# Attention accumulators split by head and half of the queries, their copy on VectorE, another phase table and a ring of fifteen score tiles

## Chip, cores and metric

The program runs on one core of a Trainium2 chip. The metric is device time in microseconds (us), the median of several executions. One further execution was recorded by the hardware profiler; all rows below come from it.

## What is computed

Four transformer layers are applied to a sequence of 2048 tokens with 576 features, all in float32. Layers 0 and 2 are multi-head attention (32 heads of width 18), layers 1 and 3 have the same queries but one key and one value head that all 32 query heads share. The reference, cut to what matters:

```python
def _A_ref(x, wqkv, wo):              # layers 0 and 2
    qkv = (x @ wqkv).reshape(B, S, 3, H, Dh) ...
    scores = jnp.einsum("bhqd,bhkd->bhqk", q, k) * (Dh ** -0.5)
    p = softmax(scores, axis=-1)
    o = jnp.einsum("bhqk,bhkd->bhqd", p, v)
    return o.reshape(B, S, D) @ wo
def _B_ref(x, wq, wk, wv, wo):        # layers 1 and 3: k, v shared by all heads
    ...
x = x + _A_ref(_layernorm(x), A_wqkv, A_wo)
x = x + _B_ref(_layernorm(x), B_wq, B_wk, B_wv, B_wo)
x = x + _A_ref(_layernorm(x), A_wqkv, A_wo)
x = x + _B_ref(_layernorm(x), B_wq, B_wk, B_wv, B_wo)
```

## The kernel before

**Work and units.** In each layer the heads are taken in 16 pairs and the queries in four blocks of 512. A pair with a block is one *unit* here; a layer has 64 of them. Within a pair, head a=0 has its operands in partitions 0 to 63 and head a=1 in partitions 64 to 127 of `big`, so a score matmul uses only half the rows of the array, and two score matmuls of different heads can run beside each other.

A unit needs three kinds of work on TensorE (PE):
- 32 tiles of 128 queries by 512 keys for the row maximum (`psm`, `max_mm`, L653). VectorE (DVE) reduces 24 of them with L658. For four pairs of them the code forms a difference tile instead (L639), ScalarE (ACT) takes its Relu into `relu` or the free part of `xo` (L651), and DVE adds that to the partner tile and takes the maximum in one operation (L656). These maxima run 14 steps ahead of the exponentials.
- 32 tiles of 128 keys by 512 queries for the exponentials (`pse`, `exp_mm`, L879). The maxima come in as two more operand rows. ACT writes exp into an SBUF tile `pt` (L883).
- The product with the values (L921): the stationary operand is a 128 by 19 block of V with a column of ones, so 19 rows come out per head and the 19th is the softmax sum. Only 32 columns of the array are needed, so four such matmuls run side by side in four column groups. All four write one PSUM bank, `oacc`, at partitions 0, 32, 64 and 96.

**The accumulators.** Before, the four column groups are (head a, parity of the key chunk). A step of 512 columns takes four `pt` tiles (two heads, two key chunks) over all 512 queries (`pv_block`). After eight steps the unit is done: ACT copies all of `oacc` into one SBUF tile `oc` (L930). GpSimd (POOL) then adds the two parities of each head (`o_sum`, L939 and L940), the reciprocal of the sum goes through DRAM and back as rows `rb` (`l_part`, `l_inv`, `l_out`, `l_rows`), POOL multiplies (`o_mul`, L962) and the rows leave to `o_d` (`o_out`, L967).

**The order.** Nothing is scheduled by a tool here: every engine runs its instructions in the order in which the code issues them. For most of a layer that order comes from the table `UNIT`, one entry per *phase*, ten phases per unit. An entry such as `("e10 m01 e00 m12 e10 m01", 320)` means: the score matmuls named there (e for an exponential tile, m for a maximum tile, r for a difference tile; then the head; then the *rank*), and after them 320 columns of the product with V. The loop at L1043 to L1055 issues them. `PV_LAG` shifts the product against the scores, so that a unit's last columns fall at the end of the table's second entry, and its copy follows there. In the last part of each layer, when all maxima are done, another loop (L1060 to L1074) takes four exponentials and 512 columns at a time.

**Buffers.** Seven PSUM banks take the score tiles. `lru` lists them from the one handed out longest ago; the rank is the place in that list from which the next tile's bank is taken, and the matmul waits until the engine that read the bank's last tile is done. `reader` notes whether that was ACT. The `pt` tiles come from a ring of 14 buffers; `slot` chooses among those whose product with V has been issued, so that ACT need not wait for its own earlier writes. A fifteenth buffer holds `oc`.

Of the kernel before, what the change touches and what calls it, by code (L numbers as in the profile page):

```python
# [17 lines left out]
DH = D // H  # L18
# [31 lines left out]
SUM_AT = 3.75  # L50
# [5 lines left out]
O_AT = 15  # L56
SOON = (11.6, 12.6, 2.9)
# [12 lines left out]
UNIT = [("e00 m10 m02 e10 e01 e10 m00", 448),  # L70
# [9 lines left out]
UNIT = [([(o[0], int(o[1]), int(o[2])) for o in rows.split()], cols) for rows, cols in UNIT]  # L80
PV_LAG = 928
# [5 lines left out]
def tile_kernel(ctx: ExitStack, tc: tile.TileContext, A_x, A_wqkv, A_wo, B_x, B_wq, B_wk, B_wv, B_wo, out):  # L87
# [58 lines left out]
    rb = cst.tile([P, 512], F32, name="rb")  # L146
# [8 lines left out]
    reader = [False] * 7  # L155
# [302 lines left out]
    for layer in range(4):  # L458
# [125 lines left out]
        mxs, nms, pts, ocs = {}, {}, {}, {}  # L584
# [38 lines left out]
        def max_mm(bank=aged):  # L623
# [9 lines left out]
            reader[lru[-1]] = False  # L633
            b, r = 64 * a, 16 * a + 4 * qc + kb
            c0 = u * 512 + qc * P
            if (p, u) >= (0, 2) and (a, qc, kb) in m_diff:
# [9 lines left out]
                reader[lru[-1]] = True  # L646
                if not by_act:
                    seen[0] = max(seen[0], wrote.get(-1 - j, -1))
                wrote[-1 - j] = ticks[0]
# [221 lines left out]
        def exp_mm(p, u, i, rank):  # L871
# [5 lines left out]
            reader[lru[-1]] = True  # L877
            r = 64 * a
            nc.tensor.matmul(e, k[r:r + KE, kc * P:(kc + 1) * P], q[r:r + KE, u * 512:(u + 1) * 512],  # L879
                             start=True, stop=True)  # L880

            pt = pts[p, u, i] = slot(by_act)
            nc.scalar.activation(pt, e, AF.Exp, scale=SCALE)  # L883

        def slot(by_act):
            n = sum(e_next)
            if n >= 1984:
                return ptile("pt")
            if len(ring) < 14:
                ring.append(ptile("pt"))  # L890
                j = len(ring) - 1
            else:
                old = [j for j in free if wrote[j] <= seen[0]]
                j = old[0] if old and not by_act else max(free, key=lambda j: wrote[j])
                if not by_act:
                    seen[0] = max(seen[0], wrote[j])
                free.remove(j)
# [6 lines left out]
        def pv_cols(cols):  # L904

            while cols:
                n, c0 = divmod(pv_at[0], 512)
                w = min(cols, 512 - c0)
# [4 lines left out]
        def pv_block(n, c0, c1):  # L913

            p, u, i = *divmod(n // STEPS, 4), n % STEPS * 4
            cs = slice(c0, c1)
            turn[0] += 1
            for i in range(i, i + 4) if turn[0] % 2 else range(i + 3, i - 1, -1):
                a, kc = (i // 2) % 2, i // 4 * 2 + i % 2
                j = 64 * a + 32 * (kc % 2)  # L920
                nc.tensor.matmul(oacc[j:j + DH + 1, cs], v_of(kc)[:, 2 * p + a if is_a else 0, :], pts[p, u, i][:, cs],  # L921
                                 start=kc < 2 and c0 == 0, stop=kc >= 14 and c1 == 512)
                if c1 == 512:
                    pt = pts.pop((p, u, i))
                    free.extend(j for j, x in enumerate(ring) if x is pt)
            if c1 == 512 and i // 4 == STEPS - 1:
                oc = ocs[p, u] = ocs["tile"]
                ticks[0] += 1
                if m_done[0] < 4 * ns:
                    nc.scalar.activation(oc, oacc, AF.Copy)  # L930
                else:
                    copy(nc.vector, oc, oacc)


        def o_sum(p, u):
            oc = ocs.pop((p, u))
            t = sums[u % 2]
            for j in (0, 64):
                copy(nc.gpsimd, t[j:j + 32], oc[j + 32:j + 64])  # L939
            nc.gpsimd.tensor_tensor(t[:96], t[:96], oc[:96], op=OP.add)  # L940

        def l_part(p, u):
            lt = lts[p, u] = pool.tile([P, 8], F32, name="lt")
            for a in range(2):
                nc.sync.dma_start(lt[64 * a:64 * a + 64, :], sums[u % 2][64 * a + DH:64 * a + DH + 1, :])
# [9 lines left out]
        def l_rows(p, u):  # L955
            for a in range(2):
                nc.sync.dma_start(rb[64 * a:64 * a + DH, :],
                                  r_d[2 * p + a:2 * p + a + 1, u * 512:(u + 1) * 512].to_broadcast([DH, 512]))

        def o_mul(p, u):  # L960
            t = sums[u % 2]
            nc.gpsimd.tensor_tensor(t[:96], t[:96], rb[:96], op=OP.mult)  # L962

        def o_out(p, u):
            for a in range(2):
                c = (2 * p + a) * DH
                nc.sync.dma_start(o_d[c:c + DH, u * 512:(u + 1) * 512], sums[u % 2][64 * a:64 * a + DH, :])  # L967
# [20 lines left out]
        for p in range(NPAIR):  # L988
            for u in range(4):
# [5 lines left out]
                for d, f in ((SUM_AT, o_sum), (L_AT, l_part), (INV_AT, l_inv), (R_AT, l_out), (RB_AT, l_rows),  # L995
# [40 lines left out]
        ocs["tile"] = ptile("oc")  # L1036

        def exp_next(a, rank=0):
            pu, kc = divmod(e_next[a], NCH)
            exp_mm(*divmod(pu, 4), kc // 2 * 4 + 2 * a + kc % 2, rank)  # L1040
# [3 lines left out]
        while m_done[0] < 4 * ns:  # L1044
            rows, cols = UNIT[phase % len(UNIT)]
            run_todo(LEAD + sum(e_next) / 4)
            for kind, a, rank in rows:
                if kind == "e":
                    exp_next(a, rank)
# [10 lines left out]
        while sum(e_next) < 4 * ns:  # L1060
# [3 lines left out]
            left, c = 4 * ns - sum(e_next), -pv_at[0] % (512 * STEPS)  # L1064
# [11 lines left out]
        for st in range(ns, ns + L_AT + 1):  # L1076
            run_todo(LEAD + st)
            if st < ns + OUT_AHEAD:
                next(outs)
                pv_cols(512 * ns - pv_at[0] - (0 if st > ns else 512))  # L1080
# [33 lines left out]
```

## Time and profile before

| | |
|---|---|
| Time, median of 3 runs (lowest to highest) | 5524.15 us (5523.9 to 5525.74) |
| Span of the profiled execution, first to last instruction | 5520.9 us |
| Granted TensorE clock | 1.000 |
| POOL busy | 1839.9 us (33%) |
| DMA, share of 16 engines, main queue | 18.7% |

The three runs carry some 3 to 5 us around the span. In the profile's rows, PE is a matmul and PEld the load of its stationary operand; a row of a timeline has the start, the time from the first start to the last end, the engine, line, operation, tiles, shapes and count. The profile counts each matmul of the product with V as two instructions, one behind the other: four matmuls of 320 columns, one for each column group, are a row with x8.

### The profile page before, as it was taken

To read this page: it belongs to the slowest core of one execution; us is meant where nothing else is said; L and a number is where in the kernel's file an instruction comes from. 1 tells how busy PE (TensorE), PEld (TensorE's weight loads), DVE (VectorE), ACT (ScalarE), POOL (GpSimd) and SP (SyncE) were. 2 spreads that over 40 slices of the span, in tenths; PEclk is the share of its full clock that TensorE was granted. 3 is DMA by queue.
4 is the path that set the end of the run, shared out by engine and by line. 5 is a ranking of instruction groups with operands and counts; after the bars stand their busy time and mean duration, and the time that the engine had idled before them with its cause. 6 is when DMAs were issued, how large, how long until landed. Compare 5 with 4: busy or idle time off the path is not lost.

```text
span 5520.9 us, 143086 instructions
## 1 busy us (share of the span) xinstructions
PE 5509.2 (100%) x55774; PEld 3050.7 (55%) x55774; DVE 4920.3 (89%) x9493; ACT 4889.3 (89%) x9882; POOL 1839.9 (33%) x2382
## 2 busy tenths in 40 slices
PE   9999999999999999999999999999999999999999
PEld 8655555454855555555686555545458545454546
DVE  4799999998799999999637999999977999999995
ACT  3599999999299999999626999999992999999996
POOL 3243333334233323233412433333342333333332
PEclk9999999999999999999999999999999999999999
DMA  6321111111411000001243211111114111010002
GB/s 219 119 60 45 45 45 48 43 45 34 136 57 31 24 24 21 24 21 25 64 176 109 58 49 43 45 46 48 40 43 133 54 28 25 24 25 21 24 15 84
DMA packets 277610, 306.04 MB, mean 55 GB/s; under 512 B 136434, under 2 KB 194378, under 8 KB 267642
## 3 DMA queue, kind: packets, MB, share of 16 engines
q1 hardware_dynamic: 276930, 296.89, 18.7%
q8 instruction: 437, 7.16, 0.5%
q14 instruction: 243, 1.99, 0.1%
HBM read 169.68 MB, written 123.13 MB: 53 GB/s over the span
## 4 chain that ended last, share of the span: by engine, by line
PE 97%; issue 1%; DVE 1%; ACT 1%; DMA 0%; POOL 0%; SPq 0%; POOLq 0%; ACTq 0%
PE oacc L921 38%; PE pse L879 27%; PE psm L653 17%; PE psn L275 7%; PE psq L481 5%; PE psm L639 3%; DVE mx L658 1%; ACT pt L883 1%; PE ps L261 0%; POOL ev L494 0%; DMA m_d<-tr 0%; DMA qk_d<-ev 0%; PE oacc L262 0%; DMA big<-m_d 0%; DMA big<-qk_d 0%
## 5 line engine op out<-in xcount | busy, mean ns | idle before, releaser
L883 ACT ACTIVATE pt<-pse 128x512 f32<-128x512 f32 x8192 | 4185.0, 612 | 10.1 <-PE pse L879 1.9
L658 DVE TENSOR_REDUCE mx<-psm 128x1 f32<-128x512 f32 x6208 | 3942.4, 684 | 88.6 <-PE psm L653 66.3
L879 PE MATMUL pse<-big 64*128 64x512 f32 x8192 | 2280.5, 432 | 0.5 <-DMA big<-m_d 0.5
L653 PE MATMUL psm<-big 62*128 62x512 f32 x7200 | 2158.9, 443 | 2.2 <-ACT evr L493 0.8
L879 PEld LDWEIGHTS pse<-big 64*128 64x128 f32 x8192 | 1174.4, 184 | 1064.2 <-ACT pt L883 758.2
L921 PE MATMUL oacc<-pt,vbuf 128*19 128x32 f32 (+11 forms) x26544 | 1728.2, 368 | 0.3 <-ACT oc L930 0.2
L653 PEld LDWEIGHTS psm<-big 62*128 62x128 f32 x7200 | 878.2, 184 | 204.3 <-DVE mx L658 75.9
L921 PEld LDWEIGHTS oacc<-pt,vbuf 128*19 128x19 f32 x26544 | 533.9, 98 | 819.9 <-issue 661.4
L186 POOL TENSOR_SCALAR hl<-neg 128x8 fp32r<-128x8 f32 x256 | 50.6, 198 | 2462.2 <-DVE neg L854 2462.2
L921 PE MATMUL oacc<-pt,vy 128*19 128x288 f32 (+3 forms) x8176 | 566.3, 383 | 0.0
L949 POOL TENSOR_TENSOR rl<-lt,mone 128x8 f32<-128x8 f32 x256 | 422.0, 1648 | 320.0 <-DMA lt<-os 318.1
L656 DVE CUSTOM_DVE_ANT_0 relu<-psm,relu 128x512 f32<-128x512 f32 x496 | 342.9, 691 | 76.3 <-ACT pt L883 50.9
L186 POOL TENSOR_SCALAR os<-oc 32x512 f32<-32x512 f32 x512 | 315.3, 616 | 102.4 <-DVE oc L186 50.6
L656 DVE CUSTOM_DVE_ANT_0 xo<-psm,xo 128x512 f32<-128x512 f32 x496 | 332.1, 670 | 15.5 <-ACT pt L883 1.6
L490 ACT ACTIVATE ev<-psq 128x512 fp32r<-128x512 f32 (+1 forms) x112 | 66.9, 597 | 311.5 <-PE psq L481 222.4
L940 POOL TENSOR_TENSOR os<-os,oc 96x512 f32<-96x512 f32 x256 | 330.6, 1291 | 21.4
L962 POOL TENSOR_TENSOR os<-os,rb 96x512 f32<-96x512 f32 x256 | 327.9, 1281 | 23.1 <-DMA rb<-r_d 23.1
L921 PEld LDWEIGHTS oacc<-pt,vy 128*19 128x19 f32 x8176 | 189.8, 98 | 242.0 <-issue 197.7
L651 ACT ACTIVATE xo<-psm 128x512 f32<-128x512 f32 x496 | 317.1, 639 | 0.0
L275 PE MATMUL psn<-wsm,xx 128*128 128x288 f32 x2240 | 310.4, 297 | 0.1
L275 PEld LDWEIGHTS psn<-wsm,xx 128*128 128x128 f32 x2240 | 299.0, 188 | 15.4 <-issue 13.1
L651 ACT ACTIVATE relu<-psm 128x512 f32<-128x512 f32 x496 | 303.6, 612 | 0.0
(102 smaller groups left out, 2781.3 us busy)
## 6 DMA issues: line engine op xcount, KB each, us to landing
big<-qk_d SPq DMA_DIRECT2D x172, 432.0 KB
qk_d<-ev SPq DMA_DIRECT2D x96, 512.0 KB
qk_d<-ev SPq DMA_DIRECT2D x120, 256.0 KB
rb<-r_d SPq DMA_DIRECT2D x512, 36.0 KB
o_d<-os SPq DMA_DIRECT2D x512, 36.0 KB
o<-o_d SPq DMA_DIRECT2D x56, 256.0 KB
xx<-qk_d SPq DMA_DIRECT2D x120, 72.0 KB
big<-m_d SPq DMA_DIRECT2D x512, 4.0 KB
```

The costliest lines, as they stand in the source:

```text
L186: eng.tensor_scalar(dst, src, 1.0, 0.0, op0=OP.mult, op1=OP.add)
L275: nc.tensor.matmul(ps, lhs[:, xc, :], wsm[:, wc, h * 288:(h + 1) * 288], start=i == 0, stop=i == len(TERMS) - 1)
L651: nc.scalar.activation(t, ps, AF.Relu)
L653: nc.tensor.matmul(ps, q[b:b + KM, c0:c0 + P], k[b:b + KM, kb * 512:(kb + 1) * 512], start=True, stop=True)
L656: nc.vector.tensor_tensor_reduce(t, ps, t, 1.0, LOWEST, OP.add, OP.max, mx[:, r:r + 1])
L658: nc.vector.reduce_max(mx[:, r:r + 1], ps, axis=AX.X)
L879: nc.tensor.matmul(e, k[r:r + KE, kc * P:(kc + 1) * P], q[r:r + KE, u * 512:(u + 1) * 512], start=True, stop=True)
L883: nc.scalar.activation(pt, e, AF.Exp, scale=SCALE)
L921: nc.tensor.matmul(oacc[j:j + DH + 1, cs], v_of(kc)[:, 2 * p + a if is_a else 0, :], pts[p, u, i][:, cs], start=kc < 2 and c0 == 0, stop=k ...
L940: nc.gpsimd.tensor_tensor(t[:96], t[:96], oc[:96], op=OP.add)
L949: nc.gpsimd.tensor_tensor(rl, lts.pop((p, u)), mone, op=OP.pow)
L962: nc.gpsimd.tensor_tensor(t[:96], t[:96], rb[:96], op=OP.mult)
```

## The change

The four column groups become (head a, half of the unit's 512 queries). A step takes two `pt` tiles (two heads, one key chunk) over 256 columns, each tile's two halves going to two groups, and a unit now has 16 such steps. Each group's accumulator is then complete over all keys, with 256 columns, so `o_sum` and the tile `oc` fall away. DVE copies `oacc[:, :256]` straight into `sums`. The sums' load becomes one DMA, the rows' store four of half the length, and `rb`, `o_mul` work on 128 partitions by 256. The table `UNIT` has other entries; the ring has 15 tiles; `reader` holds the number of ACT's last read instead of yes or no, and `slot` uses it.

The core of the diff:

```diff
+RING = 15
 UNIT = ...
-        ("m10 e00 m11 m00 e10 e01", 480),
-        ("e10 m01 e00 m12 e10 m01", 320),
-        ("e10 e01 r10 m00", 256),
+        ("e01 m11 e00 m12 e00 e10", 384),
+        ("m00 e10 m01 e10 r00 m10", 448),
+        ("e10 m01 r02 m11 e00 e11 m00", 416),
...
-PV_LAG = 928
+PV_LAG = 832
...
-            if len(ring) < 14:
+            if len(ring) < RING:
...
                 old = [j for j in free if wrote[j] <= seen[0]]
-                j = old[0] if old and not by_act else max(free, key=lambda j: wrote[j])
-                if not by_act:
+                new = [j for j in free if seen[0] < wrote[j] <= by_act]
+                if new:
+                    j = max(new, key=at_)
+                elif old and (by_act >= 0 or first or len(old) > 1):
+                    j = max(old, key=at_)
+                else:
+                    j = max(free, key=at_)
                     seen[0] = max(seen[0], wrote[j])
...
-            for i in range(i, i + 4) if turn[0] % 2 else range(i + 3, i - 1, -1):
-                a, kc = (i // 2) % 2, i // 4 * 2 + i % 2
-                j = 64 * a + 32 * (kc % 2)
-                nc.tensor.matmul(oacc[j:j + DH + 1, cs], v_of(kc)[:, 2 * p + a if is_a else 0, :], pts[p, u, i][:, cs],
-                                 start=kc < 2 and c0 == 0, stop=kc >= 14 and c1 == 512)
+            groups = [(a, h) for a in range(2) for h in range(2)]
+            for a, h in groups if turn[0] % 2 else groups[::-1]:
+                j = 64 * a + 32 * h
+                nc.tensor.matmul(oacc[j:j + DH + 1, c0:c1], v_of(kc)[:, 2 * p + a if is_a else 0, :],
+                                 pts[tiles[a]][:, 256 * h + c0:256 * h + c1],
+                                 start=kc == 0 and c0 == 0, stop=kc == NCH - 1 and c1 == 256)
...
-                if m_done[0] < 4 * ns:
-                    nc.scalar.activation(oc, oacc, AF.Copy)
-                else:
-                    copy(nc.vector, oc, oacc)
+                copy(nc.vector, sums[u % 2][:, :256], oacc[:, :256])
-        def o_sum(p, u):
-            for j in (0, 64):
-                copy(nc.gpsimd, t[j:j + 32], oc[j + 32:j + 64])
-            nc.gpsimd.tensor_tensor(t[:96], t[:96], oc[:96], op=OP.add)
```

How the order of instructions changes, at the places of which the prediction speaks. First PE, before: from the third entry of the table (its 320 columns begin a new unit in `oacc`) through the fourth and fifth.

```order
L879 MATMUL pse<-big 128x512
L653 MATMUL psm<-big 128x512
L879 MATMUL pse<-big 128x512
L653 MATMUL psm<-big 128x512
L879 MATMUL pse<-big 128x512
L653 MATMUL psm<-big 128x512
L921 MATMUL oacc<-pt,vbuf 19x320 x4
L879 MATMUL pse<-big 128x512 x2
L639 MATMUL psm<-xx,big 128x512
L653 MATMUL psm<-big 128x512
L921 MATMUL oacc<-pt,vbuf 19x192 x4
L921 MATMUL oacc<-pt,vbuf 19x64 x4
```

PE with the change, from the last score matmul of the third entry through the fourth: the first 256 columns begin a new unit.

```order
L652 MATMUL psm<-big 128x512
L927 MATMUL oacc<-pt,vbuf 19x256 x4
L927 MATMUL oacc<-pt,vbuf 19x192 x4
L877 MATMUL pse<-big 128x512
L652 MATMUL psm<-big 128x512
L639 MATMUL psm<-big 128x512
L652 MATMUL psm<-big 128x512
L877 MATMUL pse<-big 128x512 x2
L652 MATMUL psm<-big 128x512
L927 MATMUL oacc<-pt,vbuf 19x64 x4
L927 MATMUL oacc<-pt,vbuf 19x256 x4
L927 MATMUL oacc<-pt,vbuf 19x96 x4
```

The entry with four score matmuls is gone; the entries now have six or seven. A run of columns is cut wherever it crosses a multiple of 256 instead of 512, so a unit's 4096 columns come in 23 pieces instead of 17.

ACT before, around a unit's end (`oc<-oacc` is the copy, the rows of `relu` and `xo` are difference tiles):

```order
L651 ACTIVATE relu<-psm 128x512
L883 ACTIVATE pt<-pse 128x512 x8
L930 ACTIVATE oc<-oacc 128x512
L883 ACTIVATE pt<-pse 128x512 x5
L651 ACTIVATE xo<-psm 128x512
L883 ACTIVATE pt<-pse 128x512 x2
L651 ACTIVATE relu<-psm 128x512
```

ACT with the change, around a unit's end; it lies within the first row of `pt`:

```order
L650 ACTIVATE relu<-psm 128x512
L882 ACTIVATE pt<-pse 128x512 x15
L650 ACTIVATE xo<-psm 128x512
L882 ACTIVATE pt<-pse 128x512 x8
L650 ACTIVATE relu<-psm 128x512
L882 ACTIVATE pt<-pse 128x512 x8
L650 ACTIVATE xo<-psm 128x512
```

The copy has left ACT; the difference tiles stand elsewhere among the exponentials.

DVE with the change, around the copy, which is the row with `os<-oacc` (`mx` are the maxima of this unit and the next, the rows ISA the joint operations with a Relu tile):

```order
L657 TENSOR_REDUCE mx_89<-psm 128x1 x10
L655 ISA xo,mx_89<-psm,xo 128x512
L655 ISA mx_89 128x1
L657 TENSOR_REDUCE mx_89<-psm 128x1 x7
L655 ISA relu,mx_89<-psm,relu 128x512
L655 ISA mx_89 128x1
L186 TENSOR_SCALAR os_113<-oacc 128x256
L657 TENSOR_REDUCE mx_89<-psm 128x1 x2
L657 TENSOR_REDUCE mx_90<-psm 128x1
L853 TENSOR_REDUCE neg<-mx_89 128x8
L657 TENSOR_REDUCE mx_90<-psm 128x1 x2
L655 ISA xo,mx_90<-psm,xo 128x512
```

DVE before, around the end of a set of maxima (the change of `mx` and the row `neg`), had only reduces there:

```order
L658 TENSOR_REDUCE mx_89<-psm 128x1 x4
L658 TENSOR_REDUCE mx_90<-psm 128x1
L854 TENSOR_REDUCE neg<-mx_89 128x8
L658 TENSOR_REDUCE mx_90<-psm 128x1 x4
L863 STREAM_TRANSPOSE tr<-hl_115 128x32
L656 ISA xo,mx_90<-psm,xo 128x512
L656 ISA mx_90 128x1
L658 TENSOR_REDUCE mx_90<-psm 128x1 x2
```

The copy now stands behind the reduces of the second entry and ahead of those of the third.

More of the change, by code (lines that the diff above doesn't have):

```diff
@@ L144, in tile_kernel @@
     x_d = dram.tile([len(AWAY), P, D], F32, name="x_d")
-    rb = cst.tile([P, 512], F32, name="rb")
+    rb = cst.tile([P, 256], F32, name="rb")
     sums = [cst.tile([P, 512], F32, name=f"os{i}") for i in range(2)]
@@ L152, in tile_kernel @@
         nc.gpsimd.memset(t, 0.0)
-    reader = [False] * 7
+    reader = [-1] * 7
     lru, held = list(range(7)), set()
@@ L926, in pv_block @@
-            if c1 == 512 and i // 4 == STEPS - 1:
-                oc = ocs[p, u] = ocs["tile"]
-                ticks[0] += 1
-                if m_done[0] < 4 * ns:
-                    nc.scalar.activation(oc, oacc, AF.Copy)
-                else:
-                    copy(nc.vector, oc, oacc)
-        def o_sum(p, u):
-            oc = ocs.pop((p, u))
-            t = sums[u % 2]
-            for j in (0, 64):
-                copy(nc.gpsimd, t[j:j + 32], oc[j + 32:j + 64])
-            nc.gpsimd.tensor_tensor(t[:96], t[:96], oc[:96], op=OP.add)
+            tiles = [(p, u, kc // 2 * 4 + 2 * a + kc % 2) for a in range(2)]
@@ new lines, in pv_block @@
+            groups = [(a, h) for a in range(2) for h in range(2)]
[4 more added lines that the diff above has]
+                                 start=kc == 0 and c0 == 0, stop=kc == NCH - 1 and c1 == 256)
+            if c1 == 256:
+                for t in tiles:
+                    pt = pts.pop(t)
+                    free.extend(j for j, x in enumerate(ring) if x is pt)
@@ L942, in l_part @@
+            if c1 == 256 and kc == NCH - 1:
+                copy(nc.vector, sums[u % 2][:, :256], oacc[:, :256])
         def l_part(p, u):
             lt = lts[p, u] = pool.tile([P, 8], F32, name="lt")
-            for a in range(2):
-                nc.sync.dma_start(lt[64 * a:64 * a + 64, :], sums[u % 2][64 * a + DH:64 * a + DH + 1, :])
+            nc.sync.dma_start(lt, sums[u % 2][DH::32, :256])
         def l_inv(p, u):
@@ L966, in o_out @@
                 c = (2 * p + a) * DH
-                nc.sync.dma_start(o_d[c:c + DH, u * 512:(u + 1) * 512], sums[u % 2][64 * a:64 * a + DH, :])
+                for h in range(2):
+                    j, t0 = 64 * a + 32 * h, u * 512 + 256 * h
+                    nc.sync.dma_start(o_d[c:c + DH, t0:t0 + 256], sums[u % 2][j:j + DH, :256])
         relu, raw = (pool.tile([P, 640], F32, tag="xh", bufs=2, name=n) for n in ("relu", "raw"))
@@ L1046, in tile_kernel @@
             run_todo(LEAD + sum(e_next) / 4)
-            for kind, a, rank in rows:
+            for i, (kind, a, rank) in enumerate(rows):
                 if kind == "e":
-                    exp_next(a, rank)
+                    exp_next(a, rank, i < 3)
                 elif m_done[0] < 4 * ns:
```

58 lines of the change are left out of this document (30 added, 28 removed), and 6 rows, old and new, of the table UNIT.

## The prediction

> **What bounds the kernel now.** I read the page's busy times and the chain first, then busy time by stretch, then one unit on PE instruction by instruction.
>
> ```profile
> PE 5509.2 (100%) x55774; PEld 3050.7 (55%) x55774; DVE 4920.3 (89%) x9493; ACT 4889.3 (89%) x9882; POOL 1839.9 (33%) x2382
> ...
> PE oacc L921 38%; PE pse L879 27%; PE psm L653 17%; PE psn L275 7%; PE psq L481 5%; PE psm L639 3%; DVE mx L658 1%; ACT pt L883 1%; PE ps L261 0%; POOL ev L494 0%; DMA m_d<-tr 0%; DMA qk_d<-ev 0%; PE oacc L262 0%; DMA big<-m_d 0%; DMA big<-qk_d 0%
> ```
> ```profile
> core 0: us, PE busy (x) PEld busy (x) DVE busy (x) ACT busy (x) POOL busy (x), PEclk, DMA share, GB/s
> 1000.00:1036.77 36.77, 36.77 (x404) 18.47 (x400) 35.47 (x69) 36.72 (x75) 11.58 (x14) 1.00 0.14 33
> ```
>
> The chain lies on PE by 97 parts in 100, on L921, L879 and L653. But matmuls overlap in the records, so a PE that is busy all the time proves nothing, and in a stretch of two units (36.77 us) ACT is busy for 36.72 us and DVE for 35.47 us. Three engines look full. Which of them sets the pace is seen only in the starts on PE through one unit:
>
> ```profile
> 1022.44 0.50 PE L879 MATMUL pse<-big 64*128 64x512 f32 x2
> ...
> 1023.11 0.63 PE L921 MATMUL oacc<-pt,vbuf 128*19 128x192 f32 x16
> 1023.67 0.73 PE L653 MATMUL psm<-big 62*128 62x512 f32 x3
> ...
> 1024.59 1.01 PE L921 MATMUL oacc<-pt,vbuf 128*19 128x448 f32 x16
> 1025.53 0.50 PE L653 MATMUL psm<-big 62*128 62x512 f32 x1
> ...
> 1026.66 0.95 PE L921 MATMUL oacc<-pt,vbuf 128*19 128x448 f32 x8
> 1027.54 0.50 PE L879 MATMUL pse<-big 64*128 64x512 f32 x1
> ...
> 1028.67 0.90 PE L921 MATMUL oacc<-pt,vbuf 128*19 128x32 f32 x16
> 1029.50 0.50 PE L879 MATMUL pse<-big 64*128 64x512 f32 x1
> ...
> 1030.62 0.41 PE L921 MATMUL oacc<-pt,vbuf 128*19 128x128 f32 x8
> ...
> 1031.45 0.50 PE L879 MATMUL pse<-big 64*128 64x512 f32 x1
> ...
> 1032.60 0.90 PE L921 MATMUL oacc<-pt,vy 128*19 128x224 f32 x16
> 1033.43 0.50 PE L879 MATMUL pse<-big 64*128 64x512 f32 x1
> ...
> 1034.57 0.90 PE L921 MATMUL oacc<-pt,vy 128*19 128x320 f32 x16
> 1035.40 0.49 PE L879 MATMUL pse<-big 64*128 64x512 f32 x1
> ...
> 1036.53 0.95 PE L921 MATMUL oacc<-pt,vy 128*19 128x416 f32 x16
> 1037.42 0.49 PE L653 MATMUL psm<-big 62*128 62x512 f32 x1
> ...
> 1037.75 0.40 PE L653 MATMUL psm<-big 62*128 62x512 f32 x2
> ...
> 1038.33 1.00 PE L921 MATMUL oacc<-pt,vy 128*19 128x480 f32 x8
> 1039.26 0.50 PE L879 MATMUL pse<-big 64*128 64x512 f32 x1
> ...
> 1040.16 0.73 PE L921 MATMUL oacc<-pt,vbuf 128*19 128x320 f32 x8
> 1040.83 0.50 PE L879 MATMUL pse<-big 64*128 64x512 f32 x2
> ```
>
> The unit lasts 1040.83 − 1022.44 = 18.39 us. It starts at the table's fourth entry; a row of L921 with x8 is one piece of columns, x16 is two, and the shape is the first one's. From a phase's first score matmul to its first L921: with four scores 0.67 us; with six 0.92, 0.91 and 0.90 (entries 5, 2, 3); with seven 1.13, 1.13, 1.12, 1.15, 1.14 and 1.13. Two scores of different heads run together, so these are two, three and four steps, and a seventh matmul costs as much as an eighth would. The time depends on the number of steps alone, about 0.22 us each, within 0.03 us, whatever the tiles are and whoever reads them. From L921 to the next phase: 320 columns 0.67, 448 columns 0.88, 480 columns 0.93, so 0.145 us and 0.00164 us a column. In none of the ten phases is there a wait worth more than 0.02 or 0.03 us. **PE sets the pace**; ACT and DVE are full beside it because the table feeds them just enough.
>
> **The change part by part.** *Steps.* Before: one phase with two steps, three with three, six with four: 35. The new table has six phases of six scores and four of seven, heads alternating so that each still fills its pairs: 6·3 + 4·4 = 34. Taking the means of the unit above, scores cost 0.67 + 3·0.91 + 6·1.133 = 10.20 us before and 6·0.91 + 4·1.133 = 9.99 us after: **−0.21 us a unit**.
>
> *Pieces.* Columns stay 4096 a unit, and ten changes from scores to columns and back. The cuts rise from 17 pieces to 23. What a cut costs stands in pairs of rows: 448 columns in one piece take 0.88 us (from 1026.66), 416 + 32 take 0.89 (from 1036.53); 480 in one piece 0.93, 448 + 32 take 0.94 (from 1024.59). So between 0 and 0.01 us each; I take 0.005, so **+0.03 us a unit**. That covers a piece as narrow as 32, while the new ones have 64 and more. That two groups now read one `pt` tile at two places, with the same V block, appears in no row. I cost it at nothing: the columns a group streams and their number stay the same. The Trainium skill, TensorEngine Tiling (Array Packing), section Instruction Overhead, speaks against more pieces: a matmul has about 60 cycles of overhead, and one of few columns takes as long as one of 60. If 24 more matmuls, each in two passes, paid that one after the other at 2.4 GHz (the Trainium skill, TensorE: Matmul & The Clock Gate, the table at its head), it would be an estimated 1.2 us a unit, and the time an estimated 5771 us. The trace disagrees: the cut of 0.01 us above holds eight such instructions.
>
> *The copy.* From ACT goes one row a unit; DVE gets one of half the columns.
>
> ```profile
> L930 ACT ACTIVATE oc<-oacc 128x512 f32<-128x512 f32 x248 | 148.9, 600 | 0.4 <-issue 0.4
> ...
> L369 DVE TENSOR_TENSOR xo<-psn,xo 128x288 f32<-128x288 f32 x118 | 52.2, 453 | 71.8 <-PE psn L275 70.8
> ...
> L863 DVE STREAM_TRANSPOSE tr<-hl 128x32 f32<-128x32 f32 x256 | 51.4, 201 | 3.7 <-POOL hl L858 3.7
> ...
> L186 DVE TENSOR_SCALAR oc<-oacc 128x512 f32<-128x512 f32 x8 | 5.5, 691 | 6.9 <-PE oacc L921 6.3 <-POOL rl L949 0.6
> ```
>
> DVE's price for 256 columns is not there: 0.453 us for 288 and 0.691 us for 512 bound it from above, the 0.201 us of its 128x32 transpose from below. On the line through the first two it is 0.42 us, the value I take. ACT's relief is worth nothing while PE paces. DVE's load rises from 35.47/2 = 17.74 to 18.16 us a unit. That is under the new unit of 18.21 us, but barely; the busy time overstates it, since reduces that queue overlap:
>
> ```profile
> 1022.04 1.28 DVE L658 TENSOR_REDUCE mx<-psm 128x1 f32<-128x512 f32 x2
> ...
> 1031.43 6.42 DVE L658 TENSOR_REDUCE mx<-psm 128x1 f32<-128x512 f32 x10
> ```
>
> Two in 1.28 us where one alone lasts 0.68 is 0.60 us each at full pace, and ten in 6.42 is 0.64, with small waits among them. At 0.60 for the 24 reduces and four joint operations, and 0.4 for the two small ones, DVE needs 17.2 us before and 17.6 with the copy, 0.6 us less than the unit.
>
> *The added wait.* The copy waits for the unit's last product columns and stands in DVE's line ahead of the third entry's three reduces; behind these wait the PSUM banks, and PE for them. PE itself waits for the copy before it may write `oacc` again, after the third entry's six scores: a cover of 0.91 us. Copying takes 0.42, so the copy may start 0.49 us after the columns end at no cost. Two reduces stand ahead of it from the second entry. That phase lasts 0.91 + 0.145 + 384·0.00164 = 1.69 us; its two maxima start on PE at 0 and 0.33 us (1037.42 and 1037.75 in the old second entry) and take 0.5, so a DVE without arrears reduces from 0.5 to 1.7 us. It arrives at the copy about when PE does, with 0.49 us to spare, and the wait is hidden. Before, ACT's copy of 0.60 us stood at the same place, in the same cover, and the third entry still took 0.90. The copy also waits for the stores of `sums` two units before. Here are a copy and the stores issued next:
>
> ```profile
> 1002.66 0.60 ACT L930 ACTIVATE oc<-oacc 128x512 f32<-128x512 f32 x1
> ...
> 1009.81 0.81 SPq L967 DMA_DIRECT2D o_d<-os  x2
> ```
>
> These stores free the tile which the copy one unit after 1002.66 would write, at about 1021. They have 10 us to land, so that is free.
>
> *The rest.* POOL loses three operations a unit at 33% busy. SP issues one DMA more a unit, and its queue mostly waits:
>
> ```profile
> SPq L864 <- DVE mx L656: 2309.8, 242, 11.5
> ```
>
> That is 9.5 us of waiting a time. The ring of 15 and the exact readers change which buffer ACT writes and with which waits; in the unit ACT is never what PE stands for, so nothing there. At the layers' ends the eight DVE copies shrink from 0.69 to 0.42, at most 2 us in all.
>
> *Sum.* −0.21 + 0.03 = −0.18 us a unit, 18.39 to 18.21. L930 ran 248 times, 62 times a layer; the table's loop lasts until 2048 − 56 maxima are issued, 62.25 units, so 249 units in all. 249·0.18 = 45 us. The profiled span goes from 5520.9 to 5476 us. The median of the runs, 5524.15, lies 3.25 us above the span, so **5479 us**.
>
> **Bounds of that.** If cuts cost nothing and the 1.15 and 1.14 fall to 1.12 as well, it is 0.24 a unit and 60 us, with 2 us from the ends 5462. If cuts cost 0.01 each (0.15 left) and each of three more three-step phases, which lack the spare half step, waits 0.02, it is 0.09 a unit, 22 us: 5502.
>
> **The rivals.** *Partly given back:* a seven-score phase has an empty half step that takes up a late bank, a six-score phase has none, and six phases are of that kind now. For: 1.15 and 1.14 show small waits. Against: 0.92, 0.91, 0.90 show hardly any. At 0.11 to 0.14 us a unit the gain is 11 to 17 us, 5507 to 5513.
> *Nothing:* DVE's true need is nearer its busy 18.16, plus 0.1 to 0.3 us lost around the copy. The unit stays at 18.3 to 18.45: 5513 to 5535.
> *Slower, by a late copy:* if DVE comes to the copy more than 0.49 us after the columns' end, PE stands at the third entry's columns for the excess. With one reduce still ahead that is 0.11 us, with two 0.71 and (0.71 − 0.18)·249 = +132 us, 5656. For: DVE is 96% busy. Against: the count above.
> *Slower, by the pieces:* each new one pays its load of V, unhidden:
>
> ```profile
> L921 PEld LDWEIGHTS oacc<-pt,vbuf 128*19 128x19 f32 x26544 | 533.9, 98 | 819.9 <-issue 661.4 <-ACT oc L930 91.2
> ```
>
> 6·0.098 = 0.59 us, less the 0.21: +95 us, 5619. Against: the 0.01 us of a cut, which holds such loads already.
> *ACT paces:* its 36.72 of 36.77 us taken at face value. Its copy, 0.49 us from start to start (1039.46 to 1039.95, below), goes: 248·0.49 = 122 us, 5402. Against:
>
> ```profile
> 1030.04 5.02 ACT L883 ACTIVATE pt<-pse 128x512 f32<-128x512 f32 x10
> ...
> 1039.46 0.60 ACT L930 ACTIVATE oc<-oacc 128x512 f32<-128x512 f32 x1
> 1039.95 1.57 ACT L883 ACTIVATE pt<-pse 128x512 f32<-128x512 f32 x3
> ```
>
> Ten exponentials of 0.61 in 5.02 us start 0.49 apart, so 36 rows and a copy need 18.1 of 18.39 us, and PE's phases keep their lengths. The Trainium skill, Perfetto Trace Analysis, section Identifying the Most-Contended Engine, would judge PE by its weight loads, here 55%, and name ACT; the starts on PE say otherwise.
>
> **How the numbers follow.** Forecast 0.70; partly given back 0.12; nothing 0.07; late copy 0.05; pieces 0.03; ACT paces 0.03. The first two make 0.82, and their ends are the range, 5462 to 5513. A change of 0.2% (11 us) is about what can be told from none. Faster by more: 0.70 + 0.12 + 0.03 = 0.85; within: 0.07; slower: 0.08.
>
> **What would show it.** Right: units of 18.2 us; six-score phases at 0.91 and seven-score phases at 1.13; phases of three pieces within 0.02 us of the line; the copy at about 0.42 us, with the third entry's scores still 0.90 to 0.92 ahead of L921. ACT's busy share would fall by some 2%, with no further gain. Wrong: L921 waiting for the copy; six-score phases of 1.0 us; score phases unchanged but columns slower per column, which would be the two groups on one `pt` tile.

## The result, and the profile after

| | before | after |
|---|---|---|
| Time, median (lowest to highest), four executions each | 5524.02 us (5523.12 to 5525.74) | 5493.55 us (5493.19 to 5495.69) |
| Ratio, 95% interval | | 0.9945 (0.9931 to 0.996) |
| Span of the profiled execution | 5520.9 us | 5493.8 us |
| A unit: median / mean of 244, from the starts on PE | 18.382 / 18.396 us | 18.259 / 18.281 us |
| of the mean: score matmuls / product with V | 10.218 / 8.178 us | 10.072 / 8.209 us |

The changed kernel is 30.5 us faster. The forecast was 45 us faster (5479 us), its range 5462 to 5513 us. The mean unit is 0.115 us shorter, times 249 units 28.7 us; the profiled span lost 27.1 us (the profiled execution after is the longest of its four).

The page's busy times and its chain, after:

```profile
PE 5479.3 (100%) x68190; PEld 3441.6 (63%) x68190; DVE 4944.7 (90%) x9741; ACT 4810.0 (88%) x9634; POOL 1052.3 (19%) x1614
...
PE oacc L927 38%; PE pse L877 23%; PE psm L652 21%; PE psn L275 7%; PE psq L481 6%; PE psm L639 2%; DVE mx L657 1%; PE ps L261 0%; POOL ev L494 0%; DMA m_d<-tr 0%; DMA big<-m_d 0%; DMA xx<-qk_d 0%; DMA rb<-r_d 0%; PE oacc L262 0%; SPq L553 0%
```

PE still carries the chain by 97 parts in 100, POOL went from 33% to 19%, ACT from 89% to 88%, and DVE with the copy from 89% to 90%. Busy time by stretch, for one unit:

```profile
993.69:1011.94 18.25, 18.25 (x252) 10.79 (x249) 17.85 (x36) 18.03 (x37) 2.73 (x4) 1.00 0.07 18
```

The columns are PE, PEld, DVE, ACT and POOL busy. DVE works 17.85 of 18.25 us with the copy in it, where the prediction's plain sum gave 18.16; ACT 18.03. The same unit on PE, its first score matmul and first product of entries 1, 2, 3, 6, 7 and 10, with the scores between them that matter below:

```profile
993.69 0.50 PE L652 MATMUL psm<-big 62*128 62x512 f32 x1
...
994.86 0.96 PE L927 MATMUL oacc<-pt,vy 128*19 128x64 f32 x24
995.74 0.49 PE L877 MATMUL pse<-big 64*128 64x512 f32 x1
...
996.64 0.85 PE L927 MATMUL oacc<-pt,vy 128*19 128x128 f32 x16
997.42 0.50 PE L652 MATMUL psm<-big 62*128 62x512 f32 x1
...
998.33 0.95 PE L927 MATMUL oacc<-pt,vbuf 128*19 128x256 f32 x16
...
1003.14 0.49 PE L652 MATMUL psm<-big 62*128 62x512 f32 x1
1003.15 0.73 PE L877 MATMUL pse<-big 64*128 64x512 f32 x3
1003.72 0.45 PE L652 MATMUL psm<-big 62*128 62x512 f32 x2
1004.10 0.85 PE L927 MATMUL oacc<-pt,vbuf 128*19 128x256 f32 x16
1004.88 0.49 PE L877 MATMUL pse<-big 64*128 64x512 f32 x1
...
1005.78 0.85 PE L927 MATMUL oacc<-pt,vbuf 128*19 128x128 f32 x16
...
1010.03 0.50 PE L877 MATMUL pse<-big 64*128 64x512 f32 x1
...
1010.61 0.56 PE L652 MATMUL psm<-big 62*128 62x512 f32 x2
...
1011.16 0.85 PE L927 MATMUL oacc<-pt,vy 128*19 128x192 f32 x16
```

Entry 1 (seven scores) takes 1.17 us to its first product, entries 2, 3 and 7 (six) 0.90, 0.91 and 0.90, entry 6 (six) 0.96. Over the 244 units, without the three that are about 1 us or more longer (all near a layer's start), the means are 1.176, 0.898, 0.914, 1.135, 1.128, **0.953**, 0.903, 0.909, 0.908 and 1.135 us for entries 1 to 10. The forecast had 0.91 and 1.133: **two entries are 0.043 us too long each, the rest is right.** What happens in entry 6 is seen on PEld and DVE:

```profile
1002.93 0.68 DVE L655 CUSTOM_DVE_ANT_0 relu<-psm,relu 128x512 f32<-128x512 f32 x1
...
1003.49 0.36 PEld L652 LDWEIGHTS psm<-big 62*128 62x128 f32 x2
```

The last score of entry 6 takes the bank that DVE's joint operation reads, 1002.93 to 1003.61. The second of the two loads in the last row ends at 1003.85 and lasts 0.18, so it starts at 1003.67: 0.06 us after the bank is free, and only 0.05 before its matmul at 1003.72. That matmul then lasts 0.45 and the product starts 0.38 after it. In entry 7, undisturbed, the last pair starts at 1005.45, lasts 0.39, and the product follows 0.33 behind. So the *load* carries the wait for the bank; in the trace this load waits for DVE's semaphore as its matmul does. Over all 7200 matmuls of L652, a load that starts 0.2 to 0.3 us ahead (2096 of them) goes with a duration of 393 ns, one 0.10 to 0.12 ahead (319) with 393, one 0.03 to 0.06 ahead (206) with 437, one that starts at the same time (2875, mostly an entry's first pair) with 497. So for a matmul to run at full pace its bank must be free some 0.06 + 0.105 = 0.16 us before it starts. In entry 6 it is free 0.118 us before (median), in entry 1 twice 0.14 (third and seventh score, banks that ACT reads).

Not every late bank costs time. The sixth of seven scores takes a bank that is free only 0.053 to 0.063 us before in entries 1, 4, 5 and 10, and entries 4, 5 and 10 still take 1.13 us; in the kernel before it was 0.053 to 0.056 in five entries (6 to 10), which took 1.126 to 1.154. In entry 10 above, the sixth is the second matmul of 1010.61; it starts 0.49 us ahead of the product, and with faster readers (the run that shortens both, below) 0.57 ahead, while the entry takes 1.141 in place of 1.135. An entry of seven has half a step empty, and there such a wait fits in. The prediction had looked for waits of PE and saw hardly any; such a loss stands in no list of PE's waits, only in a longer matmul and a later product.

### The profile page after: what moved, and what is told of

It reads as the page before. It is cut to its first block, busy times and chain, and to the rows that moved or that the text cites. A ratio compares the mean times of both kernels' runs of the same rounds, so it can differ in the third digit from the quotient of the medians.

```text
span 5493.8 us, 166922 instructions
## 1 busy us (share of the span) xinstructions
PE 5479.3 (100%) x68190; PEld 3441.6 (63%) x68190; DVE 4944.7 (90%) x9741; ACT 4810.0 (88%) x9634; POOL 1052.3 (19%) x1614
## 4 chain that ended last, share of the span: by engine, by line
PE 97%; DMA 1%; DVE 1%; SPq 1%; POOL 0%; issue 0%; ACT 0%; POOLq 0%; ACTq 0%; DVEq 0%
PE oacc L927 38%; PE pse L877 23%; PE psm L652 21%; PE psn L275 7%; PE psq L481 6%; PE psm L639 2%; DVE mx L657 1%; PE ps L261 0%; POOL ev L494 0%; DMA m_d<-tr 0%; DMA big<-m_d 0%; DMA xx<-qk_d 0%; DMA rb<-r_d 0%; PE oacc L262 0%; SPq L553 0%
## 5 line engine op out<-in xcount | busy, mean ns | idle before, releaser
L652 PE MATMUL psm<-big 62*128 62x512 f32 x7200 | 2361.3, 438 | 1.9 <-ACT xo L650 1.1
L877 PE MATMUL pse<-big 64*128 64x512 f32 x8192 | 2358.5, 437 | 4.0 <-DMA big<-m_d 2.9
L927 PE MATMUL oacc<-pt,vbuf 128*19 128x256 f32 (+5 forms) x34864 | 1710.2, 319 | 0.1
L652 PEld LDWEIGHTS psm<-big 62*128 62x128 f32 x7200 | 1165.9, 184 | 445.9 <-ACT pt L882 342.1
L927 PEld LDWEIGHTS oacc<-pt,vbuf 128*19 128x19 f32 x34864 | 779.6, 98 | 733.2 <-issue 429.4
L927 PE MATMUL oacc<-pt,vy 128*19 128x256 f32 (+2 forms) x12272 | 570.5, 311 | 0.0
L927 PEld LDWEIGHTS oacc<-pt,vy 128*19 128x19 f32 x12272 | 277.7, 98 | 250.7 <-issue 165.1
L496 DVE TENSOR_TENSOR ev<-psq,ev 128x512 fp32r<-128x512 f32 (+1 forms) x84 | 57.9, 691 | 205.7 <-ACT ev L490 189.8
L956 POOL TENSOR_TENSOR os<-os,rb 128x256 f32<-128x256 f32 x256 | 188.1, 735 | 151.1 <-DMA rb<-r_d 96.6
L639 PE MATMUL psm<-big 54*128 54x512 f32 x512 | 204.9, 400 | 0.1
```

What stands on the lines that cost most here:

```text
L639: nc.tensor.matmul(ps.rearrange("p (h t) -> p h t", h=2) if p == 0 or not is_a else ps, q[b:b + 3 * DH, c0:c0 + P], k, start=True, stop=True)
L652: nc.tensor.matmul(ps, q[b:b + KM, c0:c0 + P], k[b:b + KM, kb * 512:(kb + 1) * 512], start=True, stop=True)
L927: nc.tensor.matmul(oacc[j:j + DH + 1, c0:c1], v_of(kc)[:, 2 * p + a if is_a else 0, :], pts[tiles[a]][:, 256 * h + c0:256 * h + c1], start ...
L956: nc.gpsimd.tensor_tensor(t, t, rb, op=OP.mult)
```

## The experiments

Times are medians; the kernel before, run on the same chips, lay between 5524.3 and 5525.8.

### Which part of the change brings the gain

T1 was: the table alone, by its one step less. Five kernels recombine the three parts: table, accumulators, engine of the copy.

**The old table in the changed kernel.**

```diff
 UNIT = ...
-        ("e01 m11 e00 m12 e00 e10", 384),
+        ("m10 e00 m11 m00 e10 e01", 480),
...
-PV_LAG = 832
+PV_LAG = 928
```

> The change without its table: accumulators by head and half of the queries, copy on VectorE, ring of 15, but the ten phases and the lag of 928 of before. Theory T1 (the table alone brings the gain; the accumulators cost 0.03 us a unit through their six more cuts, the copy nothing): a unit of 18.38 to 18.42 us against 18.38 before, so the time stays at 5524 to 5533 us. Rival T2 (taking the copy from ScalarE or the new accumulators bring part of the gain themselves): the unit falls below 18.34 and the time below 5514. Rival T3 (the new accumulators or the copy on VectorE are what took a third of the forecast gain): the unit rises to 18.43 or more, 5536 us or more.

Measured: 5565.97 us, ratio 1.0073 (1.0061 to 1.0086), unit 18.557: T3 holds, T1 missed. The product cost 0.041 us more than before, near the 0.03 of T1, but entry 3 went from 0.906 to 0.967 and entry 5 from 0.908 to 1.013. DVE around the copy in this kernel, then the same place in the changed one:

```profile
989.85 0.69 DVE L655 CUSTOM_DVE_ANT_0 relu<-psm,relu 128x512 f32<-128x512 f32 x1
990.47 0.08 DVE L655 DVE_READ_ACCUMULATOR2_ANT mx<- 128x1 f32 x1
990.47 1.28 DVE L657 TENSOR_REDUCE mx<-psm 128x1 f32<-128x512 f32 x2
991.67 0.42 DVE L186 TENSOR_SCALAR os<-oacc 128x256 f32<-128x256 f32 x1
```
```profile
996.92 0.68 DVE L655 CUSTOM_DVE_ANT_0 relu<-psm,relu 128x512 f32<-128x512 f32 x1
997.52 0.08 DVE L655 DVE_READ_ACCUMULATOR2_ANT mx<- 128x1 f32 x1
997.64 0.42 DVE L186 TENSOR_SCALAR os<-oacc 128x256 f32<-128x256 f32 x1
```

The old second entry has three maxima, the new one two, so one reduce more stands ahead of the copy. Under the old table the copy starts 0.50 us after the third entry's first score (991.17) and ends at 992.09, 0.05 ahead of the product at 992.14; in the changed kernel it starts 0.22 after (997.42) and ends 0.27 ahead of 998.33. In entry 5 the second exponential takes a bank of DVE that is free only 0.055 us before. The prediction's rival of a late copy is real; the new table is what keeps it away.

**The accumulators alone** (old table, copy of 256 columns on ACT):

```diff
-                copy(nc.vector, sums[u % 2][:, :256], oacc[:, :256])
+                copy(nc.scalar if m_done[0] < 4 * ns else nc.vector, sums[u % 2][:, :256], oacc[:, :256])
```

> The old table and lag with accumulators by head and half of the queries and a ring of 15, the copy of 256 columns on ScalarE inside the loop. T1/T5 (accumulators cost only their six more cuts, 0.03 us a unit; a shorter copy on ScalarE, 0.2 us, is worth nothing while TensorE paces): unit 18.38 to 18.43 us, time 5524 to 5536; and the 40 us lost with the copy on VectorE under the old table are the copy's alone. Rival T3 (two groups reading one score tile, or the accumulators' layout, cost more): 5540 us or more.

Measured: 5524.72 us, 0.9998 (0.9989 to 1.0007), unit 18.390. The total is as T1/T5 had it, but it is the sum of two terms that cancel: the product took 0.044 us more a unit (T1 had 0.03), and the scores 0.042 less (T1/T5 had nothing), 0.018 of it in entry 4, whose last bank, which ACT reads, was free only 0.137 us ahead before and is 0.297 ahead here. Against the kernel before, the copy on ACT is shorter here, and the ring and the choice of buffer differ too; which of these relieved the scores was not separated. The 41 us of the kernel above are the copy on DVE under a table that was not made for it.

**The new table alone**, in the kernel before:

> The kernel before with only the new table and its lag of 832: old accumulators, copy of 512 columns on ScalarE, ring of 14. T1 (34 steps in place of 35 are the gain, the copy on VectorE and the cuts are side effects): six-score phases mostly 0.91 us, unit 18.20 to 18.28 us, time 5490 to 5505. T2 (the table only works once the copy has left ScalarE, which has 36.72 us of work in two units of 36.77 and cannot follow a shorter unit): ScalarE needs 36 rows at 0.49 us and a copy of 0.49, 18.13 us a unit, but it must do so without one idle moment, so late banks take back more than half of the 0.21 us: unit 18.30 or more, 5510 us or more.

Measured: 5711.05 us, 1.0337 (1.0322 to 1.0351), unit 19.148. T1 is refuted; T2 holds, but 187 us were not foreseen by it. Waits of PE and of PEld there:

```profile
PE oacc L921 <- ACT oc L930: 121.0, 248, 0.7
```
```profile
PEld oacc L921 <- ACT oc L930: 199.0, 248, 1.2
PEld oacc L921 <- ACT pt L883: 43.9, 258, 0.2
```

Entry 3 lasts 1.471 us, 0.56 more: the new table ends a unit with four exponentials in the second entry, the copy stands behind them on ACT, and the product behind the copy. The columns of entry 5 take 1.130 in place of 0.829: they wait for score tiles that ACT has not written, 258 times. A likely reason, not tested by itself: the old accumulators open a step with four tiles at once, the new ones with two.

**The changed kernel with its copy on ACT** (same edit as for the accumulators alone), **and the new table alone with its copy of 512 columns on DVE:**

```diff
-                if m_done[0] < 4 * ns:
-                    nc.scalar.activation(oc, oacc, AF.Copy)
-                else:
-                    copy(nc.vector, oc, oacc)
+                copy(nc.vector, oc, oacc)
```

> The changed kernel with the copy of 256 columns on ScalarE again inside the ten-phase loop. Theory T5 (the new table puts ScalarE's arrears at the unit's end: the last exponential of the second entry is read 1.40 us after its score starts; a copy there stands behind it, and TensorE at the third entry's columns behind the copy): the copy ends some 4.9 us after the unit's first score, where the columns want to begin at 4.65, so the third entry lasts 1.15 to 1.30 us in place of 0.914, with more lost after it because ScalarE is late; unit 18.5 to 18.9 us, time 5560 to 5650. Rival T6 (what costs the new table 0.9 us a unit with the old accumulators is the old accumulators, not the engine of the copy): within 10 us of the changed kernel.

> The kernel before with the new table and its lag, and the copy of the whole 512 columns on VectorE (0.69 us in place of 0.42); old accumulators, ring of 14. T5 (the copy's engine decides): the copy ends some 4.52 us after the unit's first score, still before the third entry's columns at 4.65, so the third entry stays at 0.92 to 0.95; 0.27 us more work for VectorE shows as late banks in entries 4 to 7; unit 18.26 to 18.45 us, time 5490 to 5535, so 180 to 220 us under the same table with the copy on ScalarE. T6 (the accumulators decide): 5600 us or more.

Measured: copy on ACT 5586.65 us (1.0110, 1.0094 to 1.0126), entry 3 at 1.253, unit 18.630, all inside T5's ranges. The row of PE at entry 3's product names the wait:

```profile
995.58 0.41 PE L927 MATMUL oacc<-pt,vbuf 128*19 128x256 f32 x4 [0.27 <-ACT os L184]
```

New table with old accumulators and DVE's copy: 5633.82 us (1.0195, 1.018 to 1.0209), 77 us under the same table with ACT's copy where T5 had 180 to 220, and above its range. T5 was nearly right on entry 3 (0.955, against 0.92 to 0.95), but entry 4 went to 1.345, where it had foreseen small losses. DVE there:

```profile
984.26 0.69 DVE L186 TENSOR_SCALAR oc<-oacc 128x512 f32<-128x512 f32 x1
984.87 1.88 DVE L658 TENSOR_REDUCE mx<-psm 128x1 f32<-128x512 f32 x3
```

The reduces behind the copy start 0.61 us after its start, against 0.34 in the changed kernel (997.64 to 997.98), and entry 4 stands for their banks by 0.21 us. Entry 5's columns again take 1.13, and entry 7 1.00, as in the other kernel with the old accumulators: that is T6's part. Neither theory holds alone. The whole picture ("new" accumulators include the ring of 15 and the new choice of buffer):

| table | accumulators | copy | us |
|---|---|---|---|
| old | old | ACT, 512 columns | 5524.0 |
| old | new | ACT, 256 | 5524.7 |
| old | new | DVE, 256 | 5566.0 |
| new | old | ACT, 512 | 5711.1 |
| new | old | DVE, 512 | 5633.8 |
| new | new | ACT, 256 | 5586.7 |
| new | new | DVE, 256 | 5493.6 |

**Of the seven combinations run, only the one with all three parts new gains.** The old table and accumulators with the copy on DVE, that part by itself, were not run. The steps saved are the table's, but the gain comes only with the short copy on DVE and the new accumulators beside it.

### Where the missing third went

**Maxima over 448 keys** (the kernel leaves the last 64 keys of these tiles out of the maximum).

```diff
-                    nc.vector.reduce_max(mx[:, r:r + 1], ps, axis=AX.X)
+                    nc.vector.reduce_max(mx[:, r:r + 1], ps[:, :448], axis=AX.X)
```

> The changed kernel with VectorE's plain maxima taken over 448 of the 512 keys of each tile; the last 64 keys of these tiles are left out of the row maximum. Each reduce is 64 columns shorter, about 0.07 us. T1 (in the sixth entry the last score's weight load waits for a bank that VectorE frees late; in the first entry it waits for banks that ScalarE frees): entry 6 falls from 0.953 to about 0.91 us, entry 1 stays at 1.16 to 1.18, unit 18.21 to 18.23, time about 10 us less than the changed kernel's. Rival T3 (the orders of heads in these two entries cost the time by themselves, whoever reads the banks): both stay, time within 3 us of the changed kernel's. Rival T4 (ScalarE is late everywhere because VectorE's arrears delay it): both fall.

Measured: 5491.03 us, 0.9939 (0.9926 to 0.9951), unit 18.256. Entry 6 fell to 0.907, entry 1 stayed at 1.173, as T1 said; but entry 7 rose from 0.903 to 0.944, and the 10 us did not come. (The sixth score of entry 1 had its bank 0.249 us ahead here in place of 0.055, and the entry did not change: that late bank costs nothing.) PEld's waits, in this kernel and, below, in the changed one:

```profile
PEld pse L877 <- ACT pt L882: 191.5, 910, 1.1
PEld pse L877 <- DVE mx L657: 77.8, 184, 1.0
```
```profile
PEld pse L877 <- ACT pt L882: 167.0, 714, 1.4
PEld pse L877 <- DVE mx L657: 139.7, 460, 0.4
```

Waits on DVE went down by 276 times, those on ACT up by 196. In entry 7 the last exponential takes the bank of the fourth score of entry 6, which ACT reads third in line there. In the changed kernel that bank is free 0.162 us before, just enough; with entry 6 shorter, 0.111. Two banks stood at nearly the same limit.

**32 columns moved from entry 6 to entry 5:**

```diff
-        ("m02 e11 e02 m11 e00 e11 m00", 416),
-        ("m11 e00 e12 e00 m10 m01", 384),
+        ("m02 e11 e02 m11 e00 e11 m00", 448),
+        ("m11 e00 e12 e00 m10 m01", 352),
```

> The changed kernel with 32 columns moved from the sixth entry to the fifth (448 and 352), so that the sixth entry's scores start 0.053 us later after the same banks were handed to their readers. T1 (a bank must be free some 0.16 us before the matmul that overwrites it; in entry 6 it is free 0.11 us before): entry 6 falls from 0.953 to about 0.91; entries 7 to 9 start 0.05 us earlier against the engines and may give it back, so the time is between 5483 and 5495 us. Rival T3 (entry 6 costs 0.953 by its order of heads): entry 6 stays at 0.95, the time within 2 us of the changed kernel's.

Measured: 5505.61 us, 0.9964 (0.9951 to 0.9976): outside both ranges. Entry 6 fell to 0.901, so T3 is out; entry 7 rose to 1.000. The same bank explains the size. ACT begins to read entry 6's first exponential 0.57 us after the entry's start in both kernels, so the later start gives it no lead. From the entry's start to the last exponential of entry 7 it needs, by its lags in the changed kernel, 0.338 + 1.197 to the third reading, 0.61 for it and 0.16 to the matmul: 2.30 us. PE without a wait is there after 0.901 + 0.724 + 0.578 = 2.20; 0.10 us is missing, and 0.097 was lost. So entry 7 lost nearly all that entry 6 had saved (0.052 us of scores, 0.053 of columns), and the 32 columns more in entry 5 (0.058 us) were paid besides: the unit went from 18.259 to 18.311.

**Both readers shortened:** the maxima as above, and the exponentials over 448 queries (of each tile the last 64 are left out, and old values enter the product).

```diff
-            nc.scalar.activation(pt, e, AF.Exp, scale=SCALE)
+            w = 448 if any(x is pt for x in full) else 512
+            full.append(pt)
+            nc.scalar.activation(pt[:, :w], e[:, :w], AF.Exp, scale=SCALE)
```

> The changed kernel with both readers shortened: VectorE's plain maxima over 448 of 512 keys, and ScalarE's exponentials over 448 of the 512 queries of a tile once its buffer has been filled (the last 64 keys are left out of the maximum, and for the last 64 queries of each block stale exponentials enter the product). TensorE's own instructions, their order and ranks are those of the changed kernel. T1'' (entries 1, 6 and 7 wait for banks that the two readers free late, and for nothing else; shortening VectorE alone moved the wait to a bank of ScalarE): entry 1 falls from 1.176 to 1.12-1.14 us, entry 6 from 0.953 and entry 7 stay at 0.89-0.91, unit 18.13 to 18.19 us, time 5463 to 5476: the size of the step that the forecast assumed. Rival T3' (the orders of heads or TensorE's own loads cost 0.04 us in these entries): entry 1 stays at 1.16 or more and the unit above 18.22, time above 5483.

Measured: 5465.49 us, 0.9890 (0.9874 to 0.9907), unit 18.166. Entries 1, 6 and 7 are 1.142, 0.902 and 0.900 (entry 1 has a median of 1.129; a few long ones at layers' starts lift the mean); T1'' had 1.12 to 1.14 and twice 0.89 to 0.91. T3' is out. PE at entries 6 and 7:

```profile
998.40 0.50 PE L652 MATMUL psm<-big 62*128 62x512 f32 x1
998.40 0.73 PE L878 MATMUL pse<-big 64*128 64x512 f32 x3
998.97 0.40 PE L652 MATMUL psm<-big 62*128 62x512 f32 x2
999.30 0.85 PE L930 MATMUL oacc<-pt,vbuf 128*19 128x256 f32 x16
1000.08 0.49 PE L878 MATMUL pse<-big 64*128 64x512 f32 x1
...
1000.98 0.85 PE L930 MATMUL oacc<-pt,vbuf 128*19 128x128 f32 x16
```

The last pair of entry 6 lasts 0.40 in place of 0.45 and the product follows 0.33 behind. With PE's own program unchanged, the readers were worth 0.093 us a unit, 23 of the 28 us.

### A better order, the ring, the layers' starts

**Two more tables** were laid out by a count of the readers' paces. The third one's first, fifth and sixth entries:

```diff
-UNIT = [("m00 e11 r12 m00 m10 e00 e10", 448),
+UNIT = [("m10 r00 m11 e10 m01 e11 e00", 448),
...
-        ("m02 e11 e02 m11 e00 e11 m00", 416),
-        ("m11 e00 e12 e00 m10 m01", 384),
+        ("e10 m00 e00 e11 m00 m10 r00", 448),
+        ("e00 m10 m11 e01 m00 e10", 384),
```

> The changed kernel with a third table: again six entries of six scores and four of seven, and 4096 columns at the same lag, but orders and ranks laid out so that, by a count of the readers' own paces (one exponential in 0.48 us, one maximum in 0.60) and of 0.16 us from a bank's release to the matmul that overwrites it, no entry waits more than 0.02 us, save the first with 0.04. Theory T1' (what the changed kernel lacks of the forecast 0.21 us is the late banks of entries 1 and 6, and with them entry 7, nothing else): entry 6 at 0.90 to 0.92, entries 7 to 9 0.90 to 0.92, unit 18.20 to 18.23 us, time 8 to 15 us under the changed kernel. Rival T8 (ScalarE and VectorE have no more to give in a unit of 18.26, whatever the order; a loss removed in one entry comes back in another, as when the maxima were shortened): unit 18.25 or more, time not less than the changed kernel's, or more.

> As the third table, but another order reached by the same count, with the three-step entries at 0.89 to 0.91 and the first and fifth entries 0.03 to 0.04 over 1.13. T1': unit 18.20 to 18.23 us, 8 to 15 us under the changed kernel. T8: 18.25 us or more. If one of the two tables gains and the other loses, the count of banks lacks a wait, which the trace must then show.

Measured: 5520.65 us (0.9994, 0.9986 to 1.0003) and 5517.41 us (0.9985, 0.9976 to 0.9993), units 18.370 and 18.338. Entry 6 fell to 0.900 and 0.899, and entries 6 to 9 together from 3.673 to 3.645 and 3.624, as counted; but entry 1 went to 1.246 and 1.214, entry 5 to 1.201 and 1.205, where the count had some 1.16. T1' missed and T8 has the result. The cause has the same form: in the third table's entry 5 the last score's load starts at 1006.14, its matmul at 1006.17,

```profile
1006.14 0.18 PEld L639 LDWEIGHTS psm<-xx,big 54*128 54x128 f32 x1
```

and its bank, which ACT reads, is free only 0.088 us before (median). In its entry 1 the fifth and sixth scores have banks of ACT 0.139 and 0.109 us before. The count fell short by 0.04 to 0.08 us in these two entries. Whether another order reaches 18.17 us with full readers stays open; neither of these does.

**Ring of 14** (`RING = 14`):

> The changed kernel with a ring of 14 score tiles in place of 15. Theory T9 (the fifteenth tile is not needed: ScalarE chooses among the tiles whose product has been issued, and at most ten of a unit's tiles lie between exponential and product): within 5 us of the changed kernel. Rival (ScalarE then must reuse a tile whose product is not done): entries in which ScalarE waits for TensorE, 10 us or more over the changed kernel.

Measured: 5492.69 us, 0.9943 (0.9928 to 0.9958), every entry within 0.004 us of the changed kernel's, as T9 had it. The fifteenth tile brings nothing here.

**Row maxima loaded earlier** (`ROW_AT = 4`). In the changed kernel six units, most of them near a layer's start, were together 5.1 us over the median:

> The changed kernel with the load of the row maxima into the query operand issued at step 4 after its unit in place of step 5. Theory T7 (each layer's second unit waits for this load: first scores that last 2.2 to 2.7 us in place of 1.18 at 225.7, 3002.5 and 4026.0 us, and 0.35 us at 1620; 4.5 us in all): these waits go, time 3 to 4.5 us below the changed kernel. Rival: the load ends with the same store, issue time does not matter, or the queue is busy then: no change within 1.5 us.

Measured: 5498.27 us, 0.9951 (0.9938 to 0.9964): no gain, T7 is refuted. PE's waits for that load, in the changed kernel and here:

```profile
PE pse L877 <- DMA big<-m_d: 2.9, 5, 1.2
```
```profile
PE pse L877 <- DMA big<-m_d: 2.9, 2, 1.7
```

The wait moved to other units and kept its sum. Such excess also varied by itself: 3.5 us in eleven units before, 2.1 us in four with the ring of 14. Its cause wasn't settled.

## Why the prediction was right, point by point

- **PE sets the pace:** right, with a limit that the prediction lacked. The chain stays on PE, but with PE's program unchanged shorter readers gave 28 us. The Trainium skill, Perfetto Trace Analysis, section Identifying the Most-Contended Engine, goes by occupancy and by TensorE's weight loads, and would name DVE (90%; ACT 88%, weight loads 63%). The runs bear it out in part: DVE's shortening alone gave 2.5 us, both readers' 28, to a kernel whose PE is busy all the time.
- **Steps, −0.21 us a unit:** the term that was mis-sized. Measured: −0.16 (10.218 to 10.057, without the three disturbed units), mainly because entries 1 and 6 take 0.043 us each more than their steps; the other eight are together some 0.02 shorter than forecast. The sentence that failed is that the time depends on the number of steps alone, whoever reads the tiles. It held before, though five banks came free only 0.055 us ahead, because each of those was for the sixth of seven scores, where the half step took the wait up. The new table has late banks in places without that room: the last score of entry 6, and the third and seventh of entry 1. With both readers shortened it holds again (9.96 us of scores, forecast 9.99).
- **Pieces, +0.03:** right, 0.031 (under the old table 0.041 and 0.044). Entries of two pieces with 384 columns take 0.777, 416 in three pieces 0.835 against 0.830 in two: 0.005 a cut. No cost of two groups on one tile shows.
- **The copy, 0.42 us, hidden:** right; 0.424 us, entry 3 at 0.914, 0.27 us to spare where the prediction had 0.49. But the reason given, a DVE without arrears after two reduces, is a property of the new second entry: under the old one 0.05 was left, and 41 us were lost.
- **ACT's relief is worth nothing:** under the old table the total did not move (5524.7), but only because 0.042 us of scores saved met 0.044 of product; for the new table it is wrong, there the copy on ACT costs 93 us. The prediction priced the edits one by one, each against the kernel before; they are conditions of each other.
- **The ring:** nothing, right.
- **The sum:** 249 · 0.049 = 12 us of the missing 14.5 are the unit's 18.259 in place of 18.21. The time lies within the forecast's own lower bound (5502), but that bound was made of dearer cuts and of 0.02 us in each of three more entries of six. The loss came elsewhere, 0.04 us in two entries, one of them of seven; that the range held is in part luck.
- **The rival "partly given back"** named this mechanism, a late bank, and gave it to the six-score phases, because those of seven have an empty half step. The runs bear out the half step for the sixth score, but not for every bank: entry 1, of seven, lost as much as entry 6, by its third and seventh. The time fell between forecast and rival.

## What to carry to other kernels

Look for the slack of each buffer, not for waits: if an engine's operand load carries the wait, a release 0.04 us too late can cost 0.04 us in every round and need stand in no list of the engine's stalls. Where in the sequence the late buffer falls decides whether it costs anything. When several readers run nearly full, removing the nearest late release uncovers the next; test by shortening all of them at once, which gives the bound, before reordering. Price a change's parts together: here the table alone lost 187 us, the accumulators alone gained nothing, and no two parts together gained.

## What the hardware showed

Where its bank is free in time, a weight load of a score matmul starts up to 0.23 us before its matmul, while the matmul before it in the same rows of the array is still in flight (entry 7 above: both heads' matmuls run from 1004.88 to 1005.37, and the next loads start at 1004.99). The Trainium skill, TensorE: Matmul & The Clock Gate, section The mechanism, says that the queue pulls a load ahead of matmuls in flight if it is for other rows or goes to a background weight buffer. The trace fits the second case: the rows are the same here. It adds that the load waits with its matmul for the output bank: 0.05 to 0.06 us from release to load; a matmul that starts 0.1 us or more behind its load lasts 393 ns. Three times one mechanism, a bank free 0.118, 0.111 and 0.054 us ahead (entry 6; entry 7 with shorter maxima; entry 7 with moved columns), cost 0.045, 0.041 and 0.097 us: nearly all that was lacking to 0.16. At the sixth of seven scores 0.055 us ahead cost nothing.
